# A store moved from GpSimd's queue to SyncE's, and a weight load let go sooner

## The chip, the core and the metric

The kernel runs on one core of a Trainium2 chip. The metric is the time of one execution on the device, in microseconds; lower is better. Engines are named PE (TensorE, matmuls), DVE (VectorE), ACT (ScalarE), POOL (GpSimd) and SP (SyncE). SP does nothing but issue DMAs; POOL computes and issues DMAs; all DMAs run on the core's 16 DMA engines.

## The reference

The input `x` is 8 x 4224 x 192 in float32. First a causal convolution over the sequence: 8 heads of 24 channels each have 7 taps, which are the softmax of a row of `weight`. Then a feed-forward block with a residual:

```
w   = softmax(weight)                       # 8 heads x 7 taps
y   = sum over k of w[h, k] * x_pad[s + k]  # causal, per head: the "attention" output
xn  = (y - mean(y)) / sqrt(var(y) + 1e-6) * g_ln
out = y + relu(xn @ w_ch1) @ w_ch2          # 192 -> 768 -> 192
```

`w_ch1` and `w_ch2` (w1 and w2 below) arrive in float64; the kernel reads their words and puts them together as float32 on the chip.

## The kernel before

**Groups.** The rows are cut into groups. A row of the sequence belongs to a partition, and a full group holds 16 rows (`J`) on each of 128 partitions. Group 0 is 6 rows a partition, group 1 the remainder of the sequences, groups 2 to 16 are full, and the last one, 17, has 10 rows. Groups 0 and 1 are computed plainly; from group 2 on the two layers use a Strassen-like scheme of seven products (`up_mixed` for the first layer, `down_fast` for the second), which needs sums of quarters, most of them formed by DVE, some by DMAs that add.

**One group's path.** `load_x(g)` brings x by SP's queue into one of two buffers (`xg`). ACT multiplies the first two taps into `y[g]` (`first_tap`) and `tb[g]` (`second_tap`); POOL issues four DMAs that add `tb[g]` into `y[g]` (`add_in_parts`, L407); DVE adds the other taps (`conv`, L415) and transposes (`transpose`, L426). Group 2 alone has its third tap by ACT as well, and a DVE addition at L1056 that completes `y[2]`. `y[g]` is stored to `out` (`store_y`, L487), and the feed-forward part is later added to `out` in memory by DMAs of POOL (`add_to_out`, L942).

**Running ahead.** While PE works on group g, the other engines prepare group g+1: its taps on ACT and its additions on DVE stand, in the program's order, between the pieces of group g. Each engine works its instructions off in the order in which they are written (`manual_schedule`), and each DMA queue its DMAs.

**Closings.** In `up_mixed` each product goes into one half (X or Y) of the eight PSUM banks. `evict` (L635) copies a half out by ACT; `close` adds a product to a quarter already copied: by DVE straight from PSUM (L641), or by an ACT copy into a spare tile (`parts_cs`, `parts_tb`) and an adding DMA of POOL (L599). Relus by ACT (L648) follow, and `lower_sum` on DVE (L822). The second layer (L846) takes its banks when L641 and the last eviction have read them, and its left operands from the Relus.

**Where `y` is stored.** Groups 0, 1, and from 3 on store by SP. Group 2's store is issued by POOL within `up_mixed`, between two closings:

```
        p.close(p.c21, Y, two.c22[:, 0:1])
        if g == 2:
            store_y(g, nc.gpsimd)
```

**SP's queue around it.** In order: w1's words, the first x (group 0, three pieces), w2's words (L988), x of group 1, the store of `y[0]`, x of group 2, the store of `y[1]`, x of group 3, x of group 4 (the fifth x, issued when DVE's `conv(2)` has freed the buffer), the store of `y[3]`, x of group 5, and so on.

**w2's gate.** w1 is put together on DVE in three slices (`join_low`, `join_sign`, `join_product` for s = 0, 1, 2). A memset on one corner of `raw2`, the tile that receives w2's words, holds the load of w2 back until DVE has come to that place:

```
        if s == 1:
            nc.vector.memset(raw2[0:1, 0:1, :], 0)
```

x of group 1 is held in the same way by a memset behind the third slice (`gate=True`, L138). w2's first reader is L231 on DVE, behind the transposes of group 0.

Of the kernel before, what the change touches and what calls it, by code (L numbers as in the profile page):

```python
# [16 lines left out]
def kernel(  # L17
# [29 lines left out]
    nc = tc.nc  # L47
# [44 lines left out]
    def rows_of_out(g, j1, j2):  # L92

        b, j0, n = groups[g]
        if b is not None:
            return [(slice(0, P), outr[b, :, (j0 + j1) * D : (j0 + j2) * D])]
        left = out[:, P * R : S].rearrange("b (p r) d -> p b (r d)", p=LP)
        return [(slice(0, P), left[:, :, j1 * D : j2 * D])]
# [30 lines left out]
    def clear_pad(g):  # L129
        nc.gpsimd.memset(xg[g][0:1, 0:PAD, :], 0.0)  # L130

    def load_x(g, queue=nc.sync, later=False, gate=False):
        b, j0, n = groups[g]
        t = xpool.tile([P, J + PAD, D], F32, tag="xg", name=f"xg{g}")
        xg[g] = t
        flat = t.rearrange("p j d -> p (j d)")
        if gate:
            nc.vector.memset(t[0 : 1 if b is not None else P, 0:1, 0:1], 0.0)  # L138
        if b is None:
            queue.dma_start(  # L140
                out=flat[:, 0 : (PAD + n) * D],
                in_=bass.AP(
                    tensor=x.tensor, offset=(P * R - PAD) * D,
                    ap=[[n * D, LP], [S * D, B], [1, (PAD + n) * D]],
                ),
            )
            return
        if j0:
            queue.dma_start(
                out=flat[:, 0 : (n + PAD) * D], in_=xr[b, :, (j0 - PAD) * D : (j0 + n) * D]  # L150
            )
            return
        if b:

            queue.dma_start(
                out=flat[:, 0 : (PAD + n) * D],
                in_=bass.AP(
                    tensor=x.tensor, offset=(b * S - PAD) * D, ap=[[R * D, P], [1, (PAD + n) * D]]
                ),
            )  # L160
            if not later:
                clear_pad(g)
            return
        clear_pad(g)
        for p0, p1 in ((16, P), (1, 16)):
            nc.sync.dma_start(
                out=flat[p0:p1, 0 : (PAD + n) * D],
                in_=bass.AP(
                    tensor=x.tensor, offset=(b * S + p0 * R - PAD) * D,
                    ap=[[R * D, p1 - p0], [1, (PAD + n) * D]],  # L170
                ),
            )
        nc.sync.dma_start(out=flat[0:1, PAD * D : (PAD + n) * D], in_=xr[b, 0:1, 0 : n * D])
# [72 lines left out]
    def join_low(raw, mant, power):  # L246
        mant = mant.bitcast(F32)
        nc.vector.scalar_tensor_tensor(
            out=mant, in0=raw[:, :, 0], scalar=2.0**-52, in1=mant, op0=ALU.mult, op1=ALU.add
        )  # L250

    def join_sign(raw, mant, power):
        hi, power = raw[:, :, 1], power.bitcast(U32)
        nc.vector.scalar_tensor_tensor(
            out=power, in0=hi, scalar=0x80000000, in1=power,
            op0=ALU.bitwise_and, op1=ALU.bitwise_or,
        )

    def join_product(dst, raw, mant, power, g=None):
        mant, power = mant.bitcast(F32), power.bitcast(F32)  # L260
        if g is None:
            nc.vector.tensor_tensor(dst, mant, power, op=ALU.mult)
            return
        nc.vector.scalar_tensor_tensor(
            out=dst, in0=mant, scalar=g, in1=power, op0=ALU.mult, op1=ALU.mult
        )
# [142 lines left out]
    def conv(g, k0=1, k1=K, heads=(0, H)):  # L409
        n = groups[g][2]  # L410
        t = xg[g]
        for k in range(k0, k1):
            for h in range(*heads):
                cs = slice(h * GRP, h * GRP + GRP)
                nc.vector.scalar_tensor_tensor(  # L415
                    out=y[g][:, 0:n, cs], in0=t[:, k : k + n, cs], scalar=taps[:, h, k : k + 1],
                    in1=y[g][:, 0:n, cs], op0=ALU.mult, op1=ALU.add,
                )
# [65 lines left out]
    def store_y(g, queue=nc.sync):  # L484
        n = groups[g][2]
        for ps, rows in rows_of_out(g, 0, n):
            queue.dma_start(out=rows, in_=y[g][ps, 0:n].rearrange("p j d -> p (j d)"))  # L487
# [54 lines left out]
    def up(g):  # L542


        n = groups[g][2]
        hidden_tile(g)
        for f in range(NF):
            banks = take_set()
            rows_of_tiles(banks, yt[g][:, 0:n], w1[:, :, f * P : f * P + P])
            evict_up(g, f, banks[:, :, 0 : n * C])  # L550
            if g == 0 and f == 0:
                first_tap(1, heads=(0, H // 2))
            elif g == 0 and f == 1:
                copies_of_w1(1, [(q, 1) for q in range(NQ)])
                scale_power(words_2[2])
            elif g == 0 and f < 4:
                first_tap(1, heads=(2 * f, 2 * f + 2))
            between(g, f)
# [7 lines left out]
    def let_in(tile):  # L566

        nc.vector.memset(tile[0:1, 0:1, 0:1], 0.0)
# [32 lines left out]
    def up_mixed(g, ahead, pending):  # L601
# [71 lines left out]
        next(pending, None)  # L673
        p.product(Y, a22, p.t[2], False)
        p.close(p.c21, Y, two.c22[:, 0:1])
        if g == 2:
            store_y(g, nc.gpsimd)
        p.product(X, s4, p.b22, False)
        p.evict(X, p.c12, True)

# [300 lines left out]
    for s in range(3):  # L981
        if s:
            join_low(*words_1[s])
            join_sign(*words_1[s])
        join_product(w1f[:, s], *words_1[s], ga if s < 2 else gb)
        if s == 1:
            nc.vector.memset(raw2[0:1, 0:1, :], 0)
    nc.sync.dma_start(  # L988
        out=raw2.rearrange("p (c d) w -> p c (d w)", d=D),
# [16 lines left out]
    def ahead(g):  # L1006


        if results is not None:
            for half in range(2):  # L1010
                finish_fast(g - 1, half, *results)
        yield
# [3 lines left out]
    for g in range(NG):  # L1016
        last = g + 1 == NG
        if g + 2 < NG and g != 1:
            load_x(g + 2)
        if g < 2:  # L1020
            up(g)
            work = []
        else:
            work = (up_last if last else up_mixed)(g, ahead(g), pending)
            pending = iter(())
        if g == 0:
            early = CH * C // GRP
            join_low(*words_2)
            conv(1, 1, 5, heads=(0, early))
            join_sign(*words_2)  # L1030
            join_product(w2flat, *words_2)
            conv(1, 5, K, heads=(0, early))
            transpose(1, 0, CH)
            conv(1, heads=(early, H))
            first_tap(2)
            second_tap(2)
            let_in(w1sums[:, 1])
            sums_of_quarters(w1sums[:, 1], w12, w22)
            sums_of_quarters(w1sums[:, 0], w11, w1sums[:, 1])
            store_y(1)  # L1040
            load_x(3, later=True, gate=True)
            transpose(1, CH, NC)
            moments(0)
            moments(1)
            down(g)
            steps = root(0)
            next(steps)
            add_in_parts(2, tb[2], third[2])
            clear_pad(3)
            next(steps)  # L1050
            sums_of_quarters(w1sums[:, 2], w21, w1sums[:, 0])
            continue
        if g == 1:
            conv(2, 3)
            flat = [v.rearrange("p j d -> p (j d)") for v in (y[2], tb[2])]
            nc.vector.tensor_tensor(flat[0], *flat, op=ALU.add)  # L1056
            transpose(2)
            fourth_sum = sums_of_y(2, nc.gpsimd)
            nc.vector.tensor_tensor(w12, w12, w11, op=ALU.subtract)
            moments(2)  # L1060
            down(g)
            fourth_sum()
            sums_of_quarters(w2sums[:, 2], b12, b22)
            sums_of_quarters(w2sums[:, 0], b12, b11)
            sums_of_quarters(w2sums[:, 1], b22, w2sums[:, 0])
            sums_of_quarters(w2sums[:, 3], b21, w2sums[:, 1])
            continue
        if g + 3 < NG:
            store_y(g + 1)
        results = down_fast(g, work)  # L1070
        if last:
            finish_fast(g, 1, *results)
            for j in range(fast[g]):
                add(g, j, ots[g][:, j])
            store(g, 0, fast[g])
            for j in range(fast[g], groups[g][2]):
                rows = take_bank()[:, 0:D]
                down_row(rows, lambda f: rows_left[g][:, j - fast[g], f])
                add(g, j, rows)
                store(g, j, j + 1)  # L1080
        elif g % 2 == 0:
            pending = root(g)
# [30 lines left out]
```

## Time and profile before

| | us |
|---|---|
| median of 3 runs (lowest, highest) | 948.33 (947.61, 949.34) |
| the profiled execution | 948.87 |
| its span | 947.0 |
| PE busy in the span | 939.2 (99%) |
| DVE, ACT, POOL busy | 893.5, 716.4, 338.4 |
| PE on group 2 (79.48 to 135.84) | 56.36 |
| PE on group 3 (135.84 to 190.81) | 54.97 |

Times within the profile are microseconds from the start of the span. A line of the timeline gives start, length, engine, line of the kernel, operation, tiles and count; brackets give the idle time of the engine before it and what ended that. A wait for several things is put down to the one that came last by the profile, and where that had long been done, it was another, often a DMA. A slice of the window view gives, for PE, its weight loads (PEld), DVE, ACT and POOL, the busy time and the number of instructions, then PE's granted clock, the busy share of the DMA engines and GB/s. The clock was 1.00 throughout.

### The profile page before, as it was taken

Reading aid. Unit: us, or ns where it says so; the run is one execution under the profiler, and the core shown is the slowest. Engines: PE = TensorE matmul, PEld = TensorE weight load, DVE = VectorE, ACT = ScalarE, POOL = GpSimd, SP = SyncE. Lnnn points to the kernel's source line nnn. Section 1 sums busy time; section 2 is a strip of 40 time slices with the busy share of each in tenths; the row PEclk is TensorE's granted clock in tenths of the full one; section 3 lists DMA queues with packets and bytes.
Section 4 is the critical chain, followed back from the end, with each engine's and each line's share of the span. In section 5 each row is a group of like instructions: output and inputs, shape, how many; then the busy total and the mean of one; then the engine's idle time right before and its main releaser. Section 6 shows DMA issues by size and latency. Waiting matters only on the chain.

```text
span 947.0 us, 38441 instructions
## 1 busy us (share of the span) xinstructions
PE 939.2 (99%) x17096; PEld 756.4 (80%) x17096; DVE 893.5 (94%) x1492; ACT 716.4 (76%) x1275; POOL 338.4 (36%) x448
## 2 busy tenths in 40 slices
PE   9999999999999999999999999999999999999998
PEld 7999779697889969687786968778796877869687
DVE  8998999999999999999999999999999999998896
ACT  7974877879687787959778795978879597877643
POOL 1097144321724136142443217231451424331130
PEclk9999999999999999999999999999999999999999
DMA  8288897988879797897979887897978979776611
GB/s 231 97 212 191 208 255 141 253 161 205 183 154 259 144 255 146 223 195 141 258 143 249 158 225 160 174 254 136 260 146 229 178 159 223 136 110 114 113 53 61
DMA packets 37851, 170.37 MB, mean 180 GB/s; under 512 B 4149, under 2 KB 5430, under 8 KB 31671
## 3 DMA queue, kind: packets, MB, share of 16 engines
q0 software_dynamic: 30672, 104.61, 59.6%
q1 hardware_dynamic: 7008, 63.31, 18.3%
q8 instruction: 134, 2.20, 0.9%
q14 instruction: 31, 0.25, 0.1%
q10 hardware_dynamic: 6, 0.00, 0.0%
HBM read 38.93 MB, written 49.35 MB: 93 GB/s over the span
## 4 chain that ended last, share of the span: by engine, by line
PE 88%; POOL 5%; DMA 3%; DVE 2%; ACT 1%; issue 1%; POOLq 0%; ACTq 0%
PE ps L846 45%; PE ps L521 41%; DVE y L415 2%; DMA room<-room 1%; POOL d L458 1%; DMA room<-parts_cs 1%; PE ps L363 1%; POOL w1sums L571 1%; PE ps L324 1%; POOL d L476 1%; PE ps L793 0%; POOL room L407 0%; POOL room L599 0%; POOL ysums L595 0%; ACT room L635 0%
## 5 line engine op out<-in xcount | busy, mean ns | idle before, releaser
L415 DVE SCALAR_TENSOR_TENSOR y<-xg,taps,y 128x384 f32<-128x384 f32 (+3 forms) x710 | 357.2, 580 | 4.0 <-ACT room L635 3.5
L846 PE MATMUL ps<-room,w2sums 128*32 128x256 f32 (+1 forms) x4464 | 244.4, 376 | 0.5 <-issue 0.5
L635 ACT COPY room<-ps 128x512 f32<-128x512 f32 (+1 forms) x225 | 180.6, 844 | 63.2 <-PE ps L521 62.6
L521 PE MATMUL ps<-yt,w 32*128 32x256 f32 (+3 forms) x4092 | 225.8, 365 | 0.3 <-ACT room L511 0.3
L846 PEld LDWEIGHTS ps<-room,w2sums 128*32 128x32 f32 x4464 | 154.1, 110 | 84.7 <-issue 1.6
L521 PEld LDWEIGHTS ps<-yt,w 32*128 32x128 f32 x4092 | 203.7, 185 | 17.2 <-issue 6.8
L846 PE MATMUL ps<-room,w 128*32 128x256 f32 (+1 forms) x3456 | 191.8, 373 | 0.3 <-DVE room L641 0.2
L889 DVE TENSOR_TENSOR room<-room 128x1024 f32<-128x1024 f32 x135 | 154.6, 1221 | 18.1 <-PE ps L846 14.2
L846 PEld LDWEIGHTS ps<-room,w 128*32 128x32 f32 x3456 | 116.1, 110 | 67.1 <-DVE room L641 5.2
L521 PE MATMUL ps<-ysums,w1sums 32*128 32x256 f32 (+1 forms) x2304 | 132.2, 371 | 0.0
L521 PEld LDWEIGHTS ps<-ysums,w1sums 32*128 32x128 f32 x2304 | 121.5, 185 | 5.1 <-issue 0.2
L942 POOL DMA_DIRECT2D out_dram<-ot x59 | 51.0, 864 | 175.6 <-ACT ot L931 172.5
L852 ACT COPY cs<-ps 128x256 f32<-128x256 f32 (+1 forms) x192 | 70.9, 370 | 44.9 <-PE ps L846 44.5
L931 ACT ACTIVATE ot<-ot,r 128x192 f32<-128x192 f32 x238 | 101.0, 469 | 0.0
L648 ACT ACTIVATE room<-room 128x1024 f32<-128x1024 f32 x90 | 94.8, 1064 | 5.4 <-DMA room<-parts_cs 5.4
L407 POOL DMA_DIRECT2D y<-tb x59 | 52.2, 1382 | 112.1 <-ACT room L852 105.2
L376 ACT ACTIVATE y<-xg,taps 128x384 f32<-128x384 f32 (+3 forms) x141 | 72.8, 609 | 1.1 <-DMA xg<-in_x_dram 0.6
L521 PE MATMUL ps<-yt,w1sums 32*128 32x256 f32 (+1 forms) x1152 | 71.8, 371 | 0.1
L521 PE MATMUL ps<-ysums,w 32*128 32x256 f32 (+1 forms) x1152 | 71.2, 369 | 0.0
L446 DVE BATCH_NORM_STATS2 st<-y 128x6 f32<-128x192 f32 x264 | 70.2, 344 | 0.0
L852 ACT COPY room<-ps 128x256 f32<-128x256 f32 (+1 forms) x96 | 35.6, 370 | 40.9 <-PE ps L846 40.2
L384 ACT ACTIVATE tb<-xg,taps 128x384 f32<-128x384 f32 (+1 forms) x120 | 65.6, 626 | 0.0
(121 smaller groups left out, 966.6 us busy)
## 6 DMA issues: line engine op xcount, KB each, us to landing
xg<-in_x_dram SPq DMA_DIRECT2D x15, 2112.0 KB, 16.0
room<-room POOLq DMA_DIRECT2D x45, 512.0 KB, 5.1
y<-tb POOLq DMA_DIRECT2D x58, 384.0 KB, 8.5
out_dram<-ot POOLq DMA_DIRECT2D x57, 384.0 KB, 9.6
out_dram<-y SPq DMA_DIRECT2D x13, 1536.0 KB, 9.2
room<-parts_cs POOLq DMA_DIRECT2D x30, 512.0 KB, 6.9
room<-parts_tb POOLq DMA_DIRECT2D x15, 1024.0 KB, 7.6
out_dram<-y SPq DMA_DIRECT2D x2, 768.0 KB, 4.4
```

The lines of the kernel that those rows point to most:

```text
L376: nc.scalar.mul(y[g][:, 0:n, cs], xg[g][:, 0:n, cs], taps[:, h, 0:1])
L384: nc.scalar.mul(dst[:, 0:n, cs], xg[g][:, k : k + n, cs], taps[:, h, k : k + 1])
L407: nc.gpsimd.dma_start(out=ends[0], in_=ends[1], accum_op=ALU.add)
L415: nc.vector.scalar_tensor_tensor(out=y[g][:, 0:n, cs], in0=t[:, k : k + n, cs], scalar=taps[:, h, k : k + 1], in1=y[g][:, 0:n, cs], op0=AL ...
L446: nc.vector.bn_stats(out=sums[g][:, j, :], in_=y[g][:, j, :])
L521: nc.tensor.matmul(banks[:, q, i * w + j1 * t : i * w + j2 * t], right[rows, c, P * i : P * i + P], left[rows, j1:j2, c, :], start=start, ...
L635: nc.scalar.activation(to, of, AF.Relu) if relu else nc.scalar.copy(to, of)
L648: nc.scalar.activation(c, c, AF.Relu)
L846: nc.tensor.matmul(dst[C * q : C * q + C, 0:w], right[:, f, C * c : C * c + C], left[:, f, q], start=(first and f == PAIR), stop=(f == PAI ...
L852: nc.scalar.copy(to[:, c], dst[:, 0:w].rearrange("p (j t) -> p j t", t=t))
L889: nc.vector.tensor_tensor(dst[:, f], left[:, f], right_of[:, f], op=op)
L931: nc.scalar.mul(ots[g][:, j, :], ots[g][:, j, :], rstd[g][:, j : j + 1])
```

## The change

The store of `y[2]` is no longer issued by POOL within `up_mixed`. It is issued by SP in the main loop, behind the load of x of group 4 and ahead of everything of `up_mixed(2)`; what is stored is the same. And the memset that lets w2's load go stands behind the first slice of w1 instead of the second.

```diff
         p.close(p.c21, Y, two.c22[:, 0:1])
-        if g == 2:
-            store_y(g, nc.gpsimd)
         p.product(X, s4, p.b22, False)
...
         join_product(w1f[:, s], *words_1[s], ga if s < 2 else gb)
-        if s == 1:
+        if s == 0:
             nc.vector.memset(raw2[0:1, 0:1, :], 0)
...
         if g + 2 < NG and g != 1:
             load_x(g + 2)
+        if g == 2:
+            store_y(g)
         if g < 2:
```

Two lines fewer stand ahead of the main loop, so lines behind L677 have numbers lower by 2 in the changed kernel.

## The prediction

> **What bounds the kernel now.** I read the busy shares first, then the chain of work that ended last, then the timeline of groups 2 and 3, and last the DMA traffic in slices of half a microsecond.
>
> ```profile
> PE 939.2 (99%) x17096; PEld 756.4 (80%) x17096; DVE 893.5 (94%) x1492; ACT 716.4 (76%) x1275; POOL 338.4 (36%) x448
> ```
>
> TensorE (PE) has work for 939.2 of 947.0 us. Whatever makes PE wait once is added to the end, and nothing later gives it back. From 135.9 us on, the chain is PE alone. Ahead of that it runs, among others, through a DMA of group 2 (start, length, what):
>
> ```profile
> 96.48 10.87 DMA room<-parts_cs
> 107.36 0.02 issue
> 107.38 1.07 ACT room L648
> ```
>
> The closing adds of `parts_cs` land late, a Relu on ScalarE (ACT) waits, and PE waits for the Relu. The timeline shows what PE loses there:
>
> ```profile
> 87.45 14.91 DVE L415 SCALAR_TENSOR_TENSOR y<-xg,taps,y 128x384 f32<-128x384 f32 x28 [3.49 <-ACT room L635]
> ...
> 89.49 0.87 POOL L487 DMA_DIRECT2D out_dram<-y  x1
> ...
> 95.57 1.77 POOL L599 DMA_DIRECT2D room<-parts_cs  x2 [5.20 <-ACT parts_cs L635]
> ...
> 105.00 2.29 DVE L641 TENSOR_TENSOR room<-room,ps 128x2048 f32<-128x2048 f32 x1
> ...
> 107.34 4.42 PE L846 MATMUL ps<-room,w 128*32 128x256 f32 x72 [0.17 <-DVE room L641]
> 107.38 1.06 ACT L648 ACTIVATE room<-room 128x1024 f32<-128x1024 f32 x1 [1.26 <-DMA room<-parts_cs]
> ...
> 161.05 2.29 DVE L641 TENSOR_TENSOR room<-room,ps 128x2048 f32<-128x2048 f32 x1 [0.53 <-PE ps L521]
> ```
>
> Group 2 holds PE from 79.48 to 135.84 us, 56.36 us; group 3 until 190.81, 54.97. The 1.39 us between them, by the starts of PE's weight loads: 0.25 before the first product of the second layer (27.86 against 27.61), 0.33 in that product (4.03 against 3.70: the Relu), 0.67 in the next two (8.44 against 7.77: at 113.95 PE waited for "issue", nothing that the profile shows; PE's own instructions coming late over the DMA queue "instruction" is my guess), 0.14 after them. So group 2 has at most 1.39 us, 0.15%, to give back.
>
> The 0.25 us counts most below. VectorE (DVE) works without a gap from 87.45 until L641 starts at 105.00; that step frees the PSUM banks in which PE's first product begins. In group 3 the same step waited 0.53 us for PE; in group 2 it is late, and PE waits for it. So DVE has no slack here: what delays its start at 87.45 delays PE by as much. What sets that start is not the ACT step that the row names, but the four adds of `tb[3]` into `y[3]`: GpSimd issues them from 76.64 on; the last was issued at 78.33 and landed 8.7 us later, at 87.03.
>
> **The change, part by part.** *The store leaves GpSimd.* One issue of 0.87 us goes at 89.49; GpSimd then waits 5.20 us for ACT anyway, so its time is worth nothing. In the DMA engines 1.57 MB go from the stretch in which they stood ahead of the `parts_cs` adds:
>
> ```profile
> 75.00:75.50 0.50, 0.50 (x6) 0.50 (x5) 0.47 (x2) 0.00 (x0) 0.50 (x1) 1.00 0.28 83
> 75.50:76.00 0.50, 0.50 (x5) 0.50 (x5) 0.50 (x1) 0.31 (x1) 0.50 (x1) 1.00 0.00 0
> ...
> 77.50:78.00 0.50, 0.50 (x5) 0.50 (x4) 0.47 (x2) 0.00 (x0) 0.50 (x3) 1.00 0.00 0
> 78.00:78.50 0.50, 0.50 (x5) 0.50 (x4) 0.50 (x3) 0.00 (x0) 0.50 (x3) 1.00 1.11 197
> ...
> 96.00:98.00 2.00, 2.00 (x44) 1.92 (x40) 2.00 (x5) 1.34 (x2) 1.28 (x2) 1.00 1.06 379
> 98.00:100.00 2.00, 2.00 (x44) 1.91 (x40) 2.00 (x5) 2.00 (x3) 0.00 (x0) 1.00 1.01 399
> ```
>
> The last two columns are the busy share of the 16 DMA engines and GB/s. Adds run at about 200 GB/s, plain stores at about 390: the store is the hump from 96 to 100 us, 4.0 us. Without it the `parts_cs` adds land some 4 us sooner, near 103, and both Relus start as soon as ACT is free. Gain: the 0.33 us. I also count the 0.67 us as gained, because PE will now pause just before that place and its instructions can catch up; not gained is the other end.
>
> *The store enters SyncE's (SP's) queue.* It is issued behind the load of the fifth x (68.45 us), when `y[2]` is complete: L1056 runs from 68.58 for 3.40 us, so at about 72.05. A load takes about 1.0 us from issue to first bytes on this queue (w2: 10.74 to 11.75), but the fifth x still fills the engines until 75.3. Behind the store on SP stand the store of `y[3]` (114.54) and the load at 115.05: neither is held. ACT writes into the old buffer of `y[2]` at 119.89, long after. The store's bytes then flow from about 75.3 to 79.3. Until 78.0 the engines are idle today, which is 2.7 us of free cover; the last 1.3 us, 0.5 MB, fall on the adds into `y[3]`, which saturate the engines from 78.0 on. If the store begins sooner on engines that finish x early, 0.37 MB fall there.
>
> *What that costs.* The engines' work is kept, so the last add lands later by what is left of the store: 0.95 us (0.37 MB at 390 GB/s) to 1.3 us. The other bound is the row of the same four adds in later groups, which start while transfers are unfinished: in the group of 404.88 us the slots from the first bytes to the last hold 0.42 MB more than here, and the last add lands 13.4 us after the first issue, against 10.4 here: 3.0 us. But there the adds into `out` are in the remainder, ahead in the adds' own queue (one issued at 395.98 took 14.7 us to land); here there are none ahead of them. I take 1.7 us, nearer to the first bound, with 0.4 us for engines that end unevenly (from 86.0 to 86.5 the busy share was 0.45, to 87.0 still 0.12: such a tail). DVE then starts at 89.15, L641 at 106.7 and PE at 109.05: all 1.7 us go to the end.
>
> [...]
>
> *w2 one slice sooner.* The 0.06 us memset on DVE moves from 10.63 to about 9.1, so the load on SP is issued at 9.2 instead of 10.74. Nobody waits for it: its first reader L231 starts at 22.46, at the end of the transposes before it. The transfers queued behind it gain 1.5 us of lead, and their readers (ACT at 25.76 and 36.88) don't wait either. The gain is nothing. Against it: ACT waits 0.62 us for the first x at 12.18, and the start-up chain hangs on that. Its bulk has flowed by 10.25; w2's bytes would start there, beside the last small piece (10.75 to 11.0). Cost 0 to 0.3 us; I take 0.1, since the piece is ahead in the same queue.
>
> *Sum:* 1.7 − 0.33 − 0.67 + 0.1 = +0.8 us. The profiled execution took 948.87 us (span 947.0) and becomes 949.7. It lies 0.54 us above the median of the runs, 948.33, which becomes 949.1. That is less than 0.2% (1.9 us), about what a measurement of this kernel can tell from no change.
>
> **Rivals.** *DVE starts too late* (slower): the remainder costs 3.0 us, as in the later groups. For it: it is the same four adds and the same SP queue. Against: no adds into `out` here. PE then begins at 110.35: 3.0 − 1.0 + 0.1 = +2.1, 950.4; with the 0.67 us not regained, 951.1. It decides from 2.8 us on.
>
> *The adds are not held* (store and adds fit together): only the gain of 1.0 stays, 947.3. For it: the idle 2.7 us before 78.0. Against: the adds alone fill the engines (share 1.11 and 1.06).
>
> *w2 runs over the first x* (slower): if w2's share on the engine of the small piece (72 KB, 2.9 us at a sixteenth of 400 GB/s) goes ahead of it, ACT, PE and DVE start 2.9 us later: 948.33 + 2.9 − 0.1 + 0.8 = 951.9. Against: the piece is issued 5 us before, at 4.05, on the same queue.
>
> *The change doesn't do what it says:* the instruction lists show the store on SP between the fifth x and the store of `y[3]`, and the memset one slice earlier, so I give this nothing.
>
> **How the numbers follow.** Forecast 0.55, DVE too late 0.25, adds not held 0.10, w2 over x 0.06, something not seen 0.04. The range from 947.4 to 951.4 takes in the forecast, nearly all of the second case and most of the third. Slower by over 0.2%: most of the second and fourth, and some of the forecast's upper end, where the 0.67 us stays: 0.35. Faster by over 0.2% needs more than the 1.39 us that group 2 can give, so 0.07. Within: 0.58.
>
> **What would show it.** Right: traffic near 390 GB/s in 75.5 to 78.0 and none of the hump at 96; the L415 group that starts at 87.45 begins near 89.15; PE's wait for L641 near 1.9 us; no wait of L648 for `parts_cs`; first x read at about 12.2. Wrong: the L415 group at 87.5 (second rival), after 90.2 (first), or the first x read after 12.6 (third).

## The result, and the profile after

| us | before | after |
|---|---|---|
| median (lowest, highest) of 20 runs each, same chip | 949.00 (947.25, 951.27) | 950.38 (948.89, 953.90) |
| the profiled execution (its span) | 948.87 (947.0) | 953.90 (952.0) |
| PE on group 2, in the profiled execution | 56.36 | 61.93 |

The changed kernel takes 1.0018 of the time before (95% interval 1.0012 to 1.0025): 0.18% longer. The forecast was 949.1 with a range to 951.4, so the time lies in the range, 1.3 us above the forecast. The sum behind it did not hold as well as that: two things that it left out take several us, and they do not act in every execution.

The profiled execution is the longest of the 20, so it shows the full size of the effects, not the middle. PE's work is the same (939.3 us of 952.0). The timeline of the changed kernel, from the load of the fifth x to the second layer of group 2 (start, length, engine, line, operation, what ended the wait ahead of it):

```profile
70.45 0.33 SPq L149 DMA_DIRECT2D xg<-in_x_dram  x1
...
70.79 3.56 POOL L407 DMA_DIRECT2D y<-tb  x4 [2.94 <-ACT tb L384]
...
73.96 45.02 SPq L487 DMA_DIRECT2D out_dram<-y  x2
...
79.07 2.48 PEld L521 LDWEIGHTS ps<-yt,w 32*128 32x128 f32 x52 [0.22 <-issue]
...
91.57 14.91 DVE L415 SCALAR_TENSOR_TENSOR y<-xg,taps,y 128x384 f32<-128x384 f32 x28 [6.72 <-DMA y<-tb]
...
95.16 1.77 POOL L599 DMA_DIRECT2D room<-parts_cs  x2 [5.07 <-ACT parts_cs L635]
...
103.38 2.00 ACT L648 ACTIVATE room<-room 128x1024 f32<-128x1024 f32 x2
...
109.11 2.28 DVE L641 TENSOR_TENSOR room<-room,ps 128x2048 f32<-128x2048 f32 x1
111.45 0.20 PEld L844 LDWEIGHTS ps<-room,w 128*32 128x32 f32 x8 [5.10 <-DVE room L641]
111.45 6.32 PE L844 MATMUL ps<-room,w 128*32 128x256 f32 x72 [4.69 <-DVE room L641]
...
117.59 7.94 PE L844 MATMUL ps<-room,w2sums 128*32 128x256 f32 x144
```

(The line of SPq at 73.96 joins two stores: that of `y[2]` at 73.96 and that of `y[3]`, issued 45 us later.) Three things are as the prediction had them: the store is behind the fifth x on SP; the two Relus of L648 run at 103.38 without a wait; and the products with `w2sums` run in one go. But DVE starts L415 12.50 us after PE's start on group 2 (91.57 − 79.07), where it was 7.97 (87.45 − 79.48), and PE waits 4.69 us for L641.

Counted by the starts of PE's weight loads, the 5.57 us that group 2 has gained are:
- ahead of the first product of the second layer: 32.38 against 27.86, **+4.52**, which is DVE's late start (12.50 − 7.97 = 4.53);
- in that product: 5.93 against 4.03, **+1.90**;
- in the next two products: 7.76 against 8.44, **−0.68**;
- after them, 15.86 against 16.03, **−0.17**.

The first product takes longer although nothing holds it. The windows view of the same kernel shows why (PE, PEld, DVE, ACT, POOL busy; then the granted clock, DMA share, GB/s). The windows are 3.41 us long and end where the clock steps:

```profile
105.76:109.17 3.41, 0.99 (x18) 0.56 (x10) 3.41 (x7) 1.88 (x1) 0.00 (x0) 1.00 1.14 231
109.17:112.59 3.42, 1.14 (x12) 0.60 (x16) 3.32 (x3) 0.00 (x0) 0.00 (x0) 0.50 0.21 41
112.59:116.00 3.41, 3.41 (x36) 1.58 (x32) 3.41 (x7) 1.70 (x4) 0.00 (x0) 0.50 0.00 0
116.00:119.41 3.41, 3.41 (x68) 1.90 (x64) 3.28 (x6) 3.18 (x8) 1.41 (x2) 1.00 0.12 14
```

PE is busy for 0.99 us of the first window and 1.14 of the second; the window after each has half the clock. In 112.59 to 116.00 PE issues 36 matmuls, in the next window 68. PE's wait is thus paid twice: once as a wait, and again as slow products after it.

The other addition is the start of the adds into `y[3]`. In the profile of before GpSimd issued them at 76.64, behind a stretch without traffic; here it issues them at 70.79, beside the fifth x. A line of before, from its timeline, and the same step after:

```profile
57.73 10.66 DVE L415 SCALAR_TENSOR_TENSOR y<-xg,taps,y 128x384 f32<-128x384 f32 x20
...
59.81 8.65 POOL L458 TENSOR_SCALAR d<-d 128x14 f32<-128x14 f32 x1
...
68.45 0.33 SPq L149 DMA_DIRECT2D xg<-in_x_dram  x1
```

```profile
57.87 12.51 DVE L415 SCALAR_TENSOR_TENSOR y<-xg,taps,y 128x384 f32<-128x384 f32 x19
...
59.41 0.70 POOL L458 TENSOR_SCALAR d<-d 128x14 f32<-128x14 f32 x1
...
64.86 2.99 POOL L571 TENSOR_TENSOR w1sums<-w,w1sums 128x1152 f32<-128x1152 f32 x1
65.28 2.99 DVE L415 SCALAR_TENSOR_TENSOR y<-xg,taps,y 128x384 f32<-128x384 f32 x1
```

L458 is one small step of the root on GpSimd; between the start-up and this step the change alters nothing. In before it lasts 8.65 us, to 68.46, until DVE's run of L415 has ended (68.39); after, 0.70 us. There DVE's run of L415 takes longer, 12.51 us for 19 steps against 10.66 for 20, because of a single step: the last row, which is one of the 19, lasts 2.99 us, where the others last 0.60. It starts 0.42 us behind GpSimd's step of L571, which takes 2.99 us as well. So there are two timings: GpSimd **held** (the fifth x early, the adds late, an idle stretch between them) and GpSimd **free** (the fifth x some 2 us later, the adds some 6 us earlier). The experiments ask whether the change makes the difference, or the execution.

### The profile page after: what moved, and what is told of

Same layout as the page of the kernel before. It is cut to its first block, busy times and chain, and to the rows that moved or that the text cites. A ratio compares the mean times of both kernels' runs of the same rounds, so it can differ in the third digit from the quotient of the medians.

```text
span 952.0 us, 38444 instructions
## 1 busy us (share of the span) xinstructions
PE 939.3 (99%) x17096; PEld 749.1 (79%) x17096; DVE 894.6 (94%) x1492; ACT 716.5 (75%) x1275; POOL 330.6 (35%) x447
## 4 chain that ended last, share of the span: by engine, by line
PE 86%; POOL 1%; DVE 1%; DMA 1%; ACT 0%; issue 0%; ACTq 0%; POOLq 0%
PE ps L844 45%; PE ps L521 40%; DMA room<-room 1%; PE ps L791 0%; ACT room L635 0%; DVE y L415 0%; DVE room L641 0%; POOL room L599 0%; POOL d L458 0%; POOL r L481 0%; POOL d L477 0%; POOL d L476 0%; DVE room L820 0%; POOL r L458 0%; DVE y L944 0%
## 5 line engine op out<-in xcount | busy, mean ns | idle before, releaser
L415 DVE SCALAR_TENSOR_TENSOR y<-xg,taps,y 128x384 f32<-128x384 f32 (+3 forms) x710 | 359.6, 582 | 7.4 <-DMA y<-tb 6.7
L844 PEld LDWEIGHTS ps<-room,w2sums 128*32 128x32 f32 x4464 | 149.8, 110 | 87.4 <-DVE room L887 0.2
L648 ACT ACTIVATE room<-room 128x1024 f32<-128x1024 f32 x90 | 94.6, 1063 | 2.6 <-DMA room<-parts_cs 2.6
```

What stands on the lines that cost most here:

```text
L415: nc.vector.scalar_tensor_tensor(out=y[g][:, 0:n, cs], in0=t[:, k : k + n, cs], scalar=taps[:, h, k : k + 1], in1=y[g][:, 0:n, cs], op0=AL ...
L648: nc.scalar.activation(c, c, AF.Relu)
L844: nc.tensor.matmul(dst[C * q : C * q + C, 0:w], right[:, f, C * c : C * c + C], left[:, f, q], start=(first and f == PAIR), stop=(f == PAI ...
```

## The experiments

Each is timed in five rounds beside the kernel before on the same chip (the last one in one). Ratios are to that kernel, with the 95% interval; they are worked out over the rounds, and are not exactly the quotients of the medians beside them.

**1. The store alone** (w2's memset put back).

```diff
-        if s == 0:
+        if s == 1:
             nc.vector.memset(raw2[0:1, 0:1, :], 0)
```

> Only the store moves to SyncE's queue; w2's memset stays behind the second slice. Theory (the store holds the adds into y[3], DVE starts late, PE waits at L641, and where it waits long its granted clock drops): the whole of the change, 1.0 to 2.2 us over before, with runs of clock below 1.0 among them, and DVE's L415 group of group 2 starting at 88.5 to 92 us. Rival (w2's earlier load shifts the start and with it how GpSimd and VectorE fall on each other): within 0.5 us of before, clock 1.0, DVE start near 87.5.

Measured: 952.82 against 948.86, 1.0043 (1.0027 to 1.0059). One of the seven runs took 948.97, at a mean granted clock of 1.000; the six others, 951.72 to 955.81, had 0.996 to 0.998. The profiled execution is of the free timing (L458 0.71 us, adds at 71.26):

```profile
91.92 14.90 DVE L415 SCALAR_TENSOR_TENSOR y<-xg,taps,y 128x384 f32<-128x384 f32 x28 [6.61 <-DMA y<-tb]
...
111.80 5.59 PE L844 MATMUL ps<-room,w 128*32 128x256 f32 x72 [4.58 <-DVE room L641]
```

The store carries the whole loss, and it is 4.0 us by the medians where 1.0 to 2.2 were expected.

**2. w2 alone** (the store put back).

```diff
+        if g == 2:
+            store_y(g, nc.gpsimd)
...
-        if g == 2:
-            store_y(g)
```

> Only w2's memset moves; the store of y[2] stays on GpSimd. Theory: within 0.3 us of before, clock 1.0 in all runs, DVE's L415 group near 87.5 us. Rival (w2's load shifts the start): 1 to 2 us over before. First x read near 12.2 us by both.

Measured: 948.72 against 948.86, 0.9999 (0.9991 to 1.0008). w2's place is worth nothing. In this execution GpSimd is held (8.41 us), and a pause of PE inside the `w2sums` products is there as in before, 0.27 us by this row:

```profile
113.04 6.42 PE L846 MATMUL ps<-room,w2sums 128*32 128x256 f32 x113 [0.27 <-issue]
```

**3. No store of `y[2]`** (w2 as before).

```diff
-        if g == 2:
-            store_y(g)
```

> The store of y[2] is left out altogether (the output lacks y in the rows of the third group); w2's memset as before. It shows what a store at no cost would be worth. Theory: 0.3 to 1.0 us faster than before (the Relus no longer wait for parts_cs: 0.33; the unexplained 0.67 at 113.95 perhaps), DVE's L415 group near 87.5 us or sooner, clock 1.0. Rival (GpSimd's place of the store costs nothing): within 0.2 us of before.

Measured: 947.66 against 948.86, 0.9990 (0.9981 to 0.9998). By luck this execution has the free timing (L458 0.71 us, adds at 70.66), so it can be laid beside the profile after, which differs by the store. In the DMA view (issue, count, size of each, median us to landing) of no store, and then of the changed kernel:

```profile
y<-tb POOLq DMA_DIRECT2D x4, 384.0 KB, 12.5
```

```profile
y<-tb POOLq DMA_DIRECT2D x4, 384.0 KB, 16.5
out_dram<-y SPq DMA_DIRECT2D x1, 1536.0 KB
```

The adds land 4.0 us sooner without the store, by the median of the four. That is the whole of the store's 4.0 us: with the free timing no idle stretch hides any of it. And the free timing alone does no harm:

```profile
87.26 14.91 DVE L415 SCALAR_TENSOR_TENSOR y<-xg,taps,y 128x384 f32<-128x384 f32 x28 [2.56 <-ACT room L635]
...
107.14 4.09 PE L844 MATMUL ps<-room,w 128*32 128x256 f32 x72 [0.52 <-DVE room L641]
```

**4. Half the store** (rows 0 to 7 on SP as in the change, rows 8 to 15 on GpSimd at the old place).

```diff
+        if g == 2:
+            store_y(g, nc.gpsimd, HJ)
...
-            store_y(g)
+            store_y(g, j2=HJ)
```

> Rows 0 to 7 of y[2] are stored by SyncE behind the fifth x, rows 8 to 15 by GpSimd at the old place; w2's memset as before. Half the dose: 0.79 MB, 2.0 us of the engines' time, fits the 2.7 us in which they stood idle before the adds into y[3], where these begin at 78. Theory: the adds land less than half as late as with the whole store, time between before and e1, 0 to 0.8 us over before. If only whether a store stands on SyncE's queue mattered, as e1.

Measured: 948.33 against 948.86, ratio 1.0004 (0.9994 to 1.0015): no difference. Held timing: DVE starts 8.47 us after PE's start on group 2 (87.71 − 79.24), 0.50 later than in before (runs 2, 5 and 6, with nothing of the store on SP, have 8.05 to 8.30), and PE waits 0.67 us; the first product takes 4.09 us by its row, as at full clock. Half the store costs DVE at most a quarter of what the whole costs in the held timing (2.17 us, run 10), as is to be expected where the first part of it falls on idle engines. It is not always free: one of the twelve runs took 953.18 at a mean clock of 0.998.

**5. The store later** (on GpSimd, behind the last closing adds of the first layer, `parts_tb`, rather than between two closings).

```diff
         p.close(p.c22, Y, rooms[1][:, 0:PAIR])
+        if g == 2:
+            store_y(g, nc.gpsimd)
```

> The store of y[2] stays on GpSimd, but is issued behind the closing of c22 (parts_tb, near 104 us) instead of ahead of those of c11; w2's memset as before. It then flows near 111 to 115 us, when the DMA engines stood idle. Theory (a store costs only where somebody waits for adds behind it): as e3 without the store, 0.5 to 1.2 us faster than before; DVE's L415 group near 87.3 us, L648 not waiting for parts_cs. Rival (the gain of e3 came from moving 1.57 MB less, wherever): as before, within 0.3 us.

Measured: 947.77 against 948.73, 0.9990 (0.9981 to 0.9998): shorter than the kernel before, and so than the changed one. The timeline:

```profile
87.74 14.91 DVE L415 SCALAR_TENSOR_TENSOR y<-xg,taps,y 128x384 f32<-128x384 f32 x28 [3.55 <-ACT room L635]
...
104.00 2.01 ACT L648 ACTIVATE room<-room 128x1024 f32<-128x1024 f32 x2
...
104.94 0.87 POOL L487 DMA_DIRECT2D out_dram<-y  x1
105.29 2.28 DVE L641 TENSOR_TENSOR room<-room,ps 128x2048 f32<-128x2048 f32 x1
...
107.62 4.09 PE L846 MATMUL ps<-room,w 128*32 128x256 f32 x72 [0.25 <-DVE room L641]
```

DVE starts at its old time, the Relus do not wait, and the 1.5 MB flow from about 110.5 to 114.5, behind the last adds (418, 406 and 393 GB/s from 111 to 114). Group 2 takes 55.26 us, 1.10 less than before; the prediction had put the most that it could give back at 1.39.

**6. The store on ACT's queue at the old place.**

```diff
+        if g == 2:
+            store_y(g, nc.scalar)
```

> The store of y[2] stays at the old place of the program but is issued by ScalarE's queue instead of GpSimd's (issued at the place of ACT's program behind the copy of c22's part, near 87 to 89 us). Theory (when the store flows decides, not whose queue it is): within 0.5 us of before, no runs with a clock below 0.999, DVE's L415 group near 87.5 us, the parts_cs adds late as before or by up to 2 us more, since a queue of its own takes its turn beside the adds. Rival (a store on a queue beside GpSimd's holds the adds wherever it stands): 1 to 4 us over before.

Measured: 949.69 against 948.73, 1.0013 (1.0004 to 1.0021): 0.96 us more where at most 0.5 was expected, and two of the eleven runs have a clock of 0.998 where none below 0.999 was expected. DVE is on time (86.84, held), but ACT's queue has nothing to wait for, so the store is issued at 86.86 and flows beside the three adds `room<-room` that GpSimd issues from 86.25 on (348, 281 and 305 GB/s in the three slices from 88 to 94). Now those land late, 12.3 us behind their issue by the median of the three, where it is 7.1 in before:

```profile
101.77 1.87 ACT L635 COPY room<-ps 128x2048 f32<-128x2048 f32 x1 [3.02 <-DMA room<-room]
...
103.69 2.87 PE L521 MATMUL ps<-yt,w1sums 32*128 32x256 f32 x48 [2.63 <-ACT room L635]
```

On SP's queue the store delays the adds into `y[3]` (16.5 us to landing in the profile after, 12.5 in run 3 without it), on ACT's these: in both it delays the adds that it flows beside. What differs is who waits for them.

**7 and 8. DVE late, without any store in the way** (the order of before, with 24 and with 32 repeated moments of `y[2]` on DVE ahead of `conv(3)`; line numbers are higher by 4).

```diff
             moments(2)
+            moments_again(16)
+            moments_again(8)
```

> Store and memset as before; 24 of the statistics of y[2] (L446, 0.27 us each) are computed a second time on DVE, 6.4 us more work ahead of the L415 group of group 2, which then starts near 90.3 instead of 87.5 us. No DMA is changed. Theory (DVE's start sets PE's wait at L641, us for us, and the clock drops in a long wait): PE waits about 3 us, time 2 to 4 us over before, some runs with clock 0.998 or less. Rival (DVE's lateness is taken up elsewhere and the changed kernel's loss is the DMA traffic itself): under 1 us over before.

> As the kernel with 24 repeated statistics, but 32, 8.5 us more work: the L415 group starts near 92.4 us, as in the changed kernel's profile (91.57). Theory: PE waits about 5 us, its granted clock falls to 0.5 for some 6 us as in the changed kernel's profile, time 5 to 7 us over before, that is 2 to 3 us more than with 24 repeats for 2.1 us more wait if the clock drops only here. Rival (lateness taken up elsewhere): under 2 us over before.

Measured: 952.27 and 954.12 against 948.73: 1.0042 (1.0028 to 1.0056) and 1.0063 (1.0051 to 1.0075). All eleven runs have a mean clock of 0.995 to 0.998. PE's wait, of the first kernel and then of the second:

```profile
109.13 5.78 PE L850 MATMUL ps<-room,w 128*32 128x256 f32 x72 [2.83 <-DVE room L645]
```

```profile
113.93 6.22 PE L850 MATMUL ps<-room,w 128*32 128x256 f32 x72 [6.19 <-DVE room L645]
```

A late DVE alone, with no store moved, makes PE wait and then gives half the clock for 3.41 us in the first (110.00 to 113.41) and 6.83 in the second. So the slow product belongs to PE's wait and not to the store.

**9. Changed kernel, the adds into `y[3]` made late** (issued behind `transpose(2)` and two memsets of one element, which tie GpSimd to DVE there).

```diff
-        if g > 2 and heads[1] == H:
+        if g > 3 and heads[1] == H:
             add_in_parts(g, y[g], tb[g])
...
             transpose(2)
+            nc.vector.memset(w2sums[0:1, 0:1, 0:1, 0:1], 0.0)
+            nc.gpsimd.memset(w2sums[0:1, 0:1, 0:1, 0:1], 0.0)
+            add_in_parts(3, y[3], tb[3])
```

> The changed kernel, but GpSimd issues the four adds into y[3] only when DVE has transposed y[2] (a one-element memset on each of the two engines orders them), so near 76 to 78 us in every execution, also where GpSimd is free for them at 70.8. The fifth x and most of the store then flow ahead of the adds in engines that have nothing else. Theory (how much of the store is left when the adds begin sets DVE's start): DVE's L415 group at 88.3 to 90 us, PE waits 1 to 2.5 us at L641, time 0.3 to 2 us over before, most runs with clock 0.999 or more, and well below the 952.8 of the kernel with the store alone. Rival (any store on SyncE's queue there costs what the two profiles show, 4 us at DVE): as the kernel with the store alone, 2 to 4 us over before.

Measured: 951.51 against 948.45, 1.0032 (1.0023 to 1.0041); the runs spread less (950.59 to 953.15). Held timing, adds issued at 77.53, DVE start at 90.50, PE's wait 2.40 us, product 5.78. Timing the adds from DVE does not mend the change, and the clock that I had expected to stay full did not: 0.50 from 111.39 to 114.81, and one of the eleven runs alone has a mean of 1.000. The tie only brings the held timing back: the adds are issued 4.70 us behind the store (run 10: 4.65), and DVE starts 10.19 us after PE's start on group 2 (run 10: 10.14).

**10. The changed kernel once more.**

> The changed kernel once more, for a second profile. If GpSimd is held at its multiply by -0.5 (L458, over 8 us at 59 to 68 us) as in the profile of before, the adds into y[3] are issued near 76 and by the theory DVE's L415 group starts at 88.3 to 89.5 us and the time is 948.8 to 950 at clock 1.0; if not, they are issued near 71 us and it starts near 91.5, with 951 to 954 us and a clock below 0.999. The rival (chance decides the clock, not the adds) has no such tie between issue time, DVE's start and clock.

Measured: 951.79 over eight runs against 948.45, 1.0030 (1.0019 to 1.0041), 949.88 at clock 1.000 and 950.21 to 954.48 at 0.996 to 0.998. That median lies above the predicted range. This execution (950.21) is of the held timing, so it answers to the prediction's sum:

```profile
59.59 8.20 POOL L458 TENSOR_SCALAR d<-d 128x14 f32<-128x14 f32 x1
...
75.98 3.54 POOL L407 DMA_DIRECT2D y<-tb  x4
...
88.94 14.90 DVE L415 SCALAR_TENSOR_TENSOR y<-xg,taps,y 128x384 f32<-128x384 f32 x28 [5.63 <-DMA y<-tb]
...
108.82 5.78 PE L844 MATMUL ps<-room,w 128*32 128x256 f32 x72 [2.33 <-DVE room L641]
```

The same kernel thus has both timings; the change does not choose between them. DVE's start is as expected for the held timing; the full clock that was expected with it is not there (0.997), so the clock is not tied to the timing alone. Of the twelve profiled executions eight are held and four free, and both kinds are among those with the store moved.

**Which wait costs clock.** Every stretch of full clock in the traces of before and after lasts a whole multiple of 3.413 us (935.25 us in before; 102.40 and 836.27 in the profile after), and the stretches of half clock in group 2 of runs 1, 7, 8, 9 and 10 last one such window or two. So windows can be laid out for an execution without a step as well, from where its full clock begins (7.17 us in run 6). Run 10, where the step comes, and then run 6, where it does not:

```profile
106.49:109.90 3.41, 1.08 (x20) 0.68 (x24) 3.31 (x3) 1.88 (x1) 0.00 (x0) 1.00 0.95 195
109.90:113.32 3.42, 3.42 (x36) 1.70 (x32) 3.42 (x7) 2.12 (x5) 0.00 (x0) 0.50 0.01 0
113.32:116.73 3.41, 3.41 (x68) 2.08 (x64) 3.28 (x7) 3.37 (x9) 1.73 (x2) 1.00 0.32 31
```

```profile
99.33:102.74 3.41, 1.73 (x32) 1.24 (x26) 3.36 (x6) 0.97 (x1) 0.00 (x0) 1.00 1.07 204
102.74:106.16 3.42, 2.48 (x44) 2.36 (x48) 1.87 (x4) 3.42 (x3) 0.47 (x1) 1.00 0.70 134
```

Run 6's wait (2.63 us) is longer than run 10's (2.33), but it straddles two windows, which keep 1.73 and 2.48 us of work; run 10's lies inside one, which keeps 1.08. In all profiled executions here a window in group 2 with 1.14 us of PE work or less was followed by half clock, and none with 1.73 or more was. At the ends of the executions, where PE runs out of work, two windows lie closer together: 1.19 us in run 7 was followed by half clock, 1.51 in run 2 was not:

```profile
942.85:946.27 3.42, 1.19 (x8) 0.89 (x6) 1.38 (x4) 0.00 (x0) 0.00 (x0) 1.00 0.57 230
946.27:948.60 2.33, 0.00 (x0) 0.00 (x0) 0.00 (x0) 0.00 (x0) 0.00 (x0) 0.50 0.27 84
```

```profile
939.49:942.90 3.41, 1.51 (x10) 1.22 (x8) 1.74 (x6) 0.00 (x0) 0.00 (x0) 1.00 0.50 200
942.90:945.60 2.70, 0.00 (x0) 0.00 (x0) 0.00 (x0) 0.00 (x0) 0.00 (x0) 1.00 0.33 112
```

The limit, as far as these traces tell, is between, 35 to 44% of the window. Full clock began at 11.04 us of the span in before, at 6.77 in the profile after and at 7.17 in run 6, and the windows lie differently with it. So of two waits of about the same length run 10's cost clock and run 6's did not; what sets the place of the windows was not shown. For a wait of 4.5 us or more it should not matter, by an estimate from these rows: one of the windows then has at least 2.25 us of it and keeps 1.16 or less, and 1.19 was too little. The executions with such a wait all have the half clock: the free timing with the store moved (4.69 us in the profile after, 4.58 in run 1), and run 8 (6.19).

## Why the prediction was right, and where its sum was wrong

- **The step that failed: the price of PE's wait.** The sum took "all 1.7 us go to the end" and priced a wait of PE at its length. In run 10 the wait is 2.33 us, and the product behind it takes 5.38 us by weight loads, not 3.70: 1.7 us more that no term held. The rows of before could not show it, for there PE never waits that long in group 2.
- **The remainder of the store (1.7 us)** was mis-sized by less than a third where its premise held: in run 10 DVE starts 10.14 us after PE's start on group 2 against 7.97, so **2.17** (1.84 against run 2, where it is 8.30). The adds were issued at 75.98. The prediction left 0.37 to 0.5 MB of the store to fall on them. By the packets in the trace 0.87 MB were left at 77.34, when their first bytes could flow (as long behind the issue as in before), and 0.87 MB take 2.2 us at 390 GB/s; the idle stretch took less than half of the store. What did not hold is "the engines' work is kept": behind the issue of the store (71.33) the fifth x, which is ahead of it in the queue, slows down while the engines are as busy as ever. Run 10 and then before:

```profile
73.00:74.00 1.00, 1.00 (x9) 1.00 (x8) 1.00 (x1) 0.00 (x0) 0.92 (x3) 1.00 1.02 237
74.00:75.00 1.00, 1.00 (x8) 1.00 (x8) 0.96 (x2) 0.00 (x0) 1.00 (x1) 1.00 0.96 253
```

```profile
73.00:74.00 1.00, 1.00 (x8) 1.00 (x7) 1.00 (x1) 0.00 (x0) 0.74 (x4) 1.00 0.86 372
74.00:75.00 1.00, 1.00 (x8) 1.00 (x7) 1.00 (x1) 0.00 (x0) 1.00 (x2) 1.00 1.02 439
```

  Runs 4 and 9 have the same dip (237 GB/s in 74 to 75 and in 75 to 76). Why the x slows down was not shown.
- **The premise, adds "from 76.64 on", was one timing of two.** It was read off one execution. In the free timing there is no idle stretch, the store's whole 4.0 us fall on the adds (run 3 against the profile after), and DVE is 4.5 us late. The rival "DVE starts too late" priced this delay at 3.0 us by the later groups; its mechanism is what the profile after shows (91.57, past the 90.2 that the prediction gave as its sign), larger, and by a cause that it did not name.
- **The two gains came.** The Relus no longer wait: with full clock the first product takes 3.70 us by weight loads in run 5, against 4.03, which is the 0.33. The stall of 0.67 us is gone (7.76 and 7.77 against 8.44). My reason for it, that PE's pause lets its instructions catch up, is half of it. In runs 7 and 8 the store stands at its old place and the stall is gone (7.77) behind waits of 2.83 and 6.19 us; but in run 5, with the store moved, a pause of 0.25 us is enough, while in run 2, with the store at its old place, a pause of 0.50 leaves 0.47 of it. The packets of the DMA queue "instruction" in the traces fit both: of those that carry 16 KB the eleventh starts at 111.58 in before and at 110.82 in run 2, where PE stalls, but at 110.33 in run 7, where PE came to that place later, and between 104.38 and 107.37 in all the others. So the store's traffic ahead of the `parts_cs` adds seems to delay PE's instructions; that PE waits for these packets is a guess still.
- **w2 (0.1 us)**: nothing. The first x is read at 12.14 us, before at 12.18, and run 2 gives 0.9999. The rival with w2 over the first x did not occur, nor did "the adds are not held".
- **The traffic**: near 390 GB/s was expected in 75.5 to 78.0; the profile after has 399 in 73.0 to 75.5 and 295 in 75.5 to 78.0, since x is still flowing. The hump at 96 is gone (195 GB/s in 95 to 97).
- **The base.** The forecast stood on 948.33, the median of 3 runs; the 20 runs of the kernel before give 949.00. So 0.67 of the 1.3 us by which the forecast time was low come from the base, and the change itself added 1.38 us where 0.8 was forecast.

In the held timing with a step of the clock (run 10) group 2 then takes +2.16 ahead of the first product, +1.35 in it, −0.67 and −0.16 after it, 2.68 us more where +0.7 was forecast. That the median rose by no more than 1.38 us on the first chip goes with a mixture of cases: eight of the 20 runs there kept a clock of 1.000 and took 948.89 to 950.11; one, at 0.999, took 950.49; the eleven with 0.996 to 0.998 took 950.18 to 953.90. (One window at half clock is 0.002 of the mean, so 0.999 is no such window; runs of the kernel before have it too.) In run 10 only one of eight kept 1.000. So the forecast time is about that of the executions in which no window fell short. Of the eleven others the range took in six; five, of 951.41 to 953.90, lie above it. That the median fell into the range was in part luck: with the mixture of run 10's chip it would not have. Single executions also differ by about 1 us outside group 2: run 10's is 1.3 us shorter there than before's.

What stays open: what decides between the two timings of GpSimd (no run tried it); how often each comes, since only profiled executions tell; why the fifth x slows down when the store is issued behind it; and where between 1.19 and 1.51 us of work in a window the clock's limit lies.

## What to carry to other kernels

A transfer taken out of one queue is not free on another: look for the adds or loads that it will flow beside, and for who waits for them; the place that paid here (run 5) was the one behind the last adds, in a stretch with no waiting reader. A wait of a nearly always busy PE of 2.3 us and more may have to be priced twice, as its length and as up to 1.7 us for each window of half clock that follows (run 10: 2.33 us, and 1.7 in the product behind it). And before a time in one profile becomes the premise of a sum, see whether it is the same in a second execution: the engine that was held for 8 us in one was free in the next.

## What the hardware showed that I had not expected

- The clock stepped at the edges of windows of 3.41 us, which lay differently in before, in the profile after and in run 6 (full clock from 11.04, 6.77 and 7.17 us on). In group 2 and at the ends of the executions every window with 1.19 us of PE work or less was followed by one at half clock, none with 1.51 or more was. PE's wait of 4.69 us in the profile after cost two windows (109.17 to 116.00), run 10's of 2.33 us a single one.
- A GpSimd step (L458) that takes 0.70 us in the profile after lasted 8.65 us in before, beside a run of DVE's L415; the other way round, one step of L415 lasted 2.99 us instead of 0.60 in the profile after, beside a GpSimd step (L571) that had started 0.42 us before it. Why was not shown; the step in before lasted through some 16 DVE instructions, not through one.
